# Softmax denominators of four units gathered onto 64 partitions before the logarithm, and spread back by DMA

## The chip, the core and the metric

The kernel runs on one core of a Trainium2 chip. Five engines share the work. TensorE (PE in the profile, with PEld for its weight loads) multiplies matrices into PSUM. ScalarE (ACT) evaluates functions such as the exponential. VectorE (DVE) and GpSimd (POOL) do elementwise work. SyncE (SP) issues the DMAs; its instructions, like those of every engine, start in program order. The metric is the device time of one execution in microseconds (us), the median over several runs; less is better.

## The reference

The function is one transformer block. With x of 2048 tokens and 512 features, c a conditioning vector and LN a layer norm without weights:

```python
mod = silu(c) @ w_mod            # six vectors: sa, ca, ga, sb, cb, gb
h = LN(x) * (1 + ca) + sa
x = x + ga * A(h)                # A: attention, 32 heads of 16, causal, window of 256 tokens
h = LN(x) * (1 + cb) + sb
x = x + gb * B(h)                # B: LN, then an MLP that mixes tokens: 2048 -> 1792 -> 2048
```

In the attention the scores are scaled by 1/4, masked to the 256 keys up to the query, and softmaxed; the result times the values goes through the 512 x 512 matrix wo. What concerns this document is the division of the softmax: each head and query has one sum of exponentials (its denominator), and the head's 16 outputs are divided by it.

## The kernel before

**Tiles and units.** The 2048 tokens are taken as four groups G of 512. A unit is half a group (256 queries, number H = 0 to 7) and a quarter of the features (g8 = 0 to 3, which is 8 heads, 128 partitions): 32 units, named (H, g8) below. The scores of the units are cut into 75 chunks of 4 x 512 columns, numbered 0 to 74. For a chunk `S` multiplies keys with queries into PSUM: three banks (`pss`, one buffer) and a fourth bank (`psb`, two buffers). `EA` and `EB` are the exponentials of the three banks and of the fourth on ScalarE, into an `et` tile of a ring of E_BUFS = 7. `M` multiplies by the mask on VectorE. When the last chunk of a unit is masked, the `AV` operations sum the unit in PSUM: `unit["ps"][:, 0, :]` gets the exponentials times the values, and `unit["ps"][:, 1, :]` gets their plain sums through the matrix of ones `ones_bd`, so that the sum of a head stands on all 16 partitions of that head.

**The division.** `finish` ends a unit. ScalarE takes the logarithm of the 128 x 256 sums out of PSUM (`ln`) and the exponential of its negative (`rz`), and VectorE multiplies (`OT`). Since a head's 16 partitions hold the same sum, each value is worked out 16 times:

```python
ac.activation(out=unit["lz"][:], in_=unit["ps"][:, 1, :], func=ACT.Ln)
ac.activation(out=unit["lz"][:], in_=unit["lz"][:], func=ACT.Exp, scale=-1.0)
ve.tensor_tensor(out=OT..., in0=unit["ps"][:, 0, :], in1=unit["lz"][:], op=ALU.mult)
```

The bank of the unit is one of three (`od0` to `od2`) that all dense products use in turn; it is held until `OT` is done.

**Work beside the attention.** `proj` makes the keys, queries and values of the next group (normalized tiles `xn`, DMA transposes `xt` into `h1T`, products `k`, `q`, `v`, copies `ke`, `qe`, `ve` out of PSUM, `kk`, `vo`, `vp` that place them). `post` takes a finished group through wo (`wo`), the residual (`x2`) and the two norms into `hb`. `partials` starts the first product of the MLP with what is there of hb (`p`, w1 loaded as `w1a` to `w1d`), and `tail` ends it (`u`, Gelu `g`) and runs the second product (`py`). `mod_ops` are the six vectors' use: four of them are broadcast to 128 partitions by products with a replicated silu(c) (`bc`) and copied out of PSUM (`bce`).

**The order.** Every operation is an `Op` with engines it may run on, a planned cost, dependencies and extra landing time. `ORDER` is a list of the operations' numbers, the result of a search; `CHOSEN` gives the engine of those that may run on two. `run_schedule` emits them in that order, so on each engine, and on SP's queue of DMAs, they run in the order of the list. SP waits at a DMA whose data is not ready, and what follows it in the list waits with it.

The names that the change touches: `finish`, `mod_ops`, `E_BUFS`, the tiles `hb`, `nothing`, `kb`, `vb`, `vs`, `sT_rep`, the operation `rel` (which frees the pool with the first weights), `ORDER` and `CHOSEN`. Most instructions are issued through one helper, so that their line is L256 in the profile; they are told apart by the tiles they write and read.

Of the kernel before, what the change touches and what calls it, by code (L numbers as in the profile page):

```python
# [59 lines left out]
E_BUFS = 7  # L60
LOG = None
ORDER = [
# [153 lines left out]
def kernel(  # L216
# [324 lines left out]
    for n, (v, dst) in enumerate(((2, bc_ga), (4, bc_cb1), (3, bc_sb), (5, bc_gb))):  # L541
        def e_bc(n, v=v):
            if n == 0:
                box["bc", v] = bank([P, D], F32, "ps_b")
# [32 lines left out]
    def norm_ops(tag, tiles, deps, poss, key, quiet):  # L577
# [32 lines left out]
        if quiet:  # L610
            return op(f"{tag}ag", "POOL", 3.1, e_ag, deps=st_ops, pos=poss[-1])
# [823 lines left out]
```

## Time and profile before

| | |
|---|---|
| time, three runs | 253.68, 253.95, 254.43 us; median 253.95 |
| span of the profiled execution | 252.3 us, first to last instruction |
| median less that span | 1.65 us |
| busy: PE, DVE, ACT, POOL | 235.3, 205.4, 179.5, 126.3 us |
| DMA | 28.13 MB, 39.4% of 16 engines' span on SP's queue |
| granted TensorE clock | 1.00 |

The profile gives the span of its execution, and no other time for it; the time of a run is the longer of the two, by what lies before the first and after the last instruction. The busy time of an engine says how long it worked, not whether the end waits for it. For that one reads the chain that ended last, the time between two like instructions of an engine, and the busy time by stretches of the span. A duration in the rows is that of one instruction from start to end; the next one of the same engine can start before that end, so the distance of two starts is often shorter.

### The profile page before, as it was taken

To read this page: it belongs to the slowest core of one execution; us is meant where nothing else is said; L and a number is where in the kernel's file an instruction comes from. 1 tells how busy PE (TensorE), PEld (TensorE's weight loads), DVE (VectorE), ACT (ScalarE), POOL (GpSimd) and SP (SyncE) were. 2 spreads that over 40 slices of the span, in tenths; PEclk is the share of its full clock that TensorE was granted. 3 is DMA by queue.
4 is the path that set the end of the run, shared out by engine and by line. 5 is a ranking of instruction groups with operands and counts; after the bars stand their busy time and mean duration, and the time that the engine had idled before them with its cause. 6 is when DMAs were issued, how large, how long until landed. Compare 5 with 4: busy or idle time off the path is not lost.

```text
span 252.3 us, 9189 instructions
## 1 busy us (share of the span) xinstructions
PE 235.3 (93%) x3949; PEld 126.0 (50%) x3949; DVE 205.4 (81%) x408; ACT 179.5 (71%) x254; POOL 126.3 (50%) x228
## 2 busy tenths in 40 slices
PE   7988888899987889999999999999999999999995
PEld 2656644445554544555546454556444444444443
DVE  5499998989989998999897999999978764444443
ACT  4699998999999999999999999997147510000000
POOL 8268968795899989845886348173000000000000
PEclk9999999999999999999999999999999999999999
DMA  6999364356055200003401536314999201111111
GB/s 200 323 351 294 48 47 86 44 70 187 3 74 112 53 23 3 4 3 104 131 3 45 155 82 189 105 44 113 343 388 386 108 22 43 44 52 52 42 44 42
DMA packets 42625, 28.13 MB, mean 111 GB/s; under 512 B 12376, under 2 KB 38488, under 8 KB 42584
## 3 DMA queue, kind: packets, MB, share of 16 engines
q1 hardware_dynamic: 42576, 27.54, 39.4%
q8 instruction: 31, 0.51, 0.9%
q14 instruction: 10, 0.08, 0.1%
q10 hardware_dynamic: 8, 0.00, 0.0%
HBM read 22.03 MB, written 2.10 MB: 96 GB/s over the span
## 4 chain that ended last, share of the span: by engine, by line
PE 52%; ACT 24%; DVE 7%; DMA 5%; issue 5%; POOL 4%; SPq 1%; POOLq 0%; DVEq 0%
ACT et L256 20%; PE py L256 19%; PE pu L256 16%; PE po L256 5%; PE pss L256 5%; ACT lz L256 3%; PE pa L256 3%; DMA x<-in_A_x_dram 2%; DVE et L256 2%; DMA h1T<-xn 2%; DMA wmod<-in_w_mod_dram 1%; POOL h1T L256 1%; PE pq L256 1%; DVE st L256 1%; PE pk L256 1%
## 5 line engine op out<-in xcount | busy, mean ns | idle before, releaser
L256 ACT ACTIVATE et<-pss 128x1536 bf16<-128x1536 f32 x75 | 110.7, 1476 | 2.8 <-PE psb L256 2.3
L256 PE MATMUL py<-guT,w2r 128*128 128x512 bf16 (+2 forms) x238 | 48.7, 366 | 0.0
L256 ACT ACTIVATE et<-psb 128x512 bf16<-128x512 f32 x75 | 46.9, 626 | 0.0
L256 DVE TENSOR_TENSOR et<-et,maskt 128x1024 bf16<-128x1024 bf16 (+2 forms) x79 | 46.4, 603 | 0.1
L256 PE MATMUL pu<-hb,w1s 128*32 128x512 bf16 (+1 forms) x302 | 39.0, 380 | 0.2 <-DVE QT L256 0.2
L256 PEld LDWEIGHTS <-w2r 128*128 128x128 bf16 x238 | 22.8, 98 | 26.1 <-issue 0.3
L256 PE MATMUL pss<-QT,KT 32*128 32x64 bf16 (+3 forms) x720 | 29.9, 230 | 6.2 <-ACT et L256 3.5
L256 PE MATMUL po<-et,VT 128*32 128x64 bf16 (+3 forms) x960 | 32.2, 234 | 1.3 <-DVE kb L256 0.6
L256 PE MATMUL po<-et,ones_bd 128*32 128x256 bf16 (+3 forms) x624 | 31.7, 268 | 0.0
L256 PEld LDWEIGHTS <-KT 32*128 32x128 bf16 x960 | 17.1, 92 | 28.5 <-issue 24.6
L256 DVE TENSOR_TENSOR otile<-py,xr 128x512 bf16<-128x512 f32 (+2 forms) x17 | 11.2, 660 | 24.4 <-PE py L256 24.2
L256 POOL TENSOR_SCALAR KT<-kb,mask_par 128x512 bf16<-128x512 bf16 (+1 forms) x36 | 25.0, 707 | 11.4 <-DVE kb L256 11.1
L256 PE MATMUL psb<-QT,KT 32*128 32x64 bf16 (+3 forms) x240 | 29.3, 231 | 0.0
L256 PEld LDWEIGHTS <-VT 128*32 128x32 bf16 x960 | 20.8, 96 | 13.2 <-issue 4.7
L256 PE MATMUL pk<-h1T,wqkv 128*32 128x512 bf16 (+4 forms) x228 | 21.1, 340 | 2.4 <-DVE OT L256 1.0
L256 DVE BATCH_NORM_STATS2 st<-x 128x6 f32<-128x512 bf16 x32 | 21.5, 680 | 2.1 <-DMA x<-in_A_x_dram 2.1
L256 PEld LDWEIGHTS <-wqkv 128*32 128x32 bf16 (+1 forms) x350 | 15.3, 96 | 12.7 <-issue 4.7
L256 PEld LDWEIGHTS <-w1s 128*32 128x32 bf16 (+1 forms) x302 | 14.1, 97 | 15.0 <-issue 1.5
L256 PE MATMUL pv<-wqkv,h1T 128*32 128x512 bf16 (+2 forms) x202 | 17.1, 348 | 1.3 <-DVE OT L256 0.7
L256 PE MATMUL pu<-hb,w1r 128*128 128x512 bf16 (+1 forms) x96 | 17.9, 380 | 0.0
L256 PE MATMUL pa<-wod,OT 128*32 128x512 bf16 (+1 forms) x136 | 17.2, 381 | 0.0
L256 PEld LDWEIGHTS <-ones_bd 128*32 128x32 bf16 x624 | 15.8, 97 | 0.1
(109 smaller groups left out, 350.1 us busy)
## 6 DMA issues: line engine op xcount, KB each, us to landing
w2r<-in_B_w_dram SPq DMA_DIRECT2D x14, 512.0 KB, 10.2
w1s<-in_B_w_dram SPq DMA_DIRECT2D x19, 256.0 KB, 4.0
w1r<-in_B_w_dram SPq DMA_DIRECT2D x9, 256.0 KB, 4.3
x<-in_A_x_dram SPq DMA_DIRECT2D x16, 128.0 KB, 5.2
wmod<-in_w_mod_dram SPq DMA_DIRECT2D x4, 512.0 KB, 7.8
out_dram<-otile SPq DMA_DIRECT2D x15, 128.0 KB, 1.7
wmod<-in_w_mod_dram SPq DMA_DIRECT2D x4, 256.0 KB, 3.9
wqkv<-in_A_wqkv_dram SPq DMA_DIRECT2D x4, 256.0 KB, 5.7
```

Source lines behind the costliest of these rows:

```text
L256: ins = call(*args, **kwargs)
```

## The change

The division is done for four units at once. `ev` copies a unit's whole PSUM tile (sums and products, 128 x 512 float32) into SBUF, on VectorE or ScalarE. `zg`, a DMA, takes every eighth partition of the sums (16 rows, one KB each) into 16 rows of a tile `zc`. When four units are in (64 rows), one `ln` and one `rz` work on those 64 x 256. `zb`, a DMA a unit, spreads the 16 rows to 128 partitions again, and `OT` multiplies from SBUF, on VectorE or GpSimd. There are seven such batches of four units and one of two; the last two units, (7,2) and (7,3), keep a logarithm and exponential of their own. `zc` has two halves in turn, and the `ev` tiles are a ring of six.

```diff
     def finish(unit, i):
         G, Hh, g8 = unit["G"], unit["H"], unit["g8"]
         av = av_ops[G, g8] = unit["avs"][-1]
-        lz_tag = turn("lz")
-
-        def e_ln(e):
-            unit["lz"] = late.tile([P, HQ], F32, name="lz", tag=lz_tag, bufs=1)
-            ac.activation(out=unit["lz"][:], in_=unit["ps"][:, 1, :], func=ACT.Ln)
-
-        def e_rz(e):
-            ac.activation(out=unit["lz"][:], in_=unit["lz"][:], func=ACT.Exp, scale=-1.0)
+        tag = turn("ev", EV_BUFS)
+        direct = Hh == 2 * NG - 1 and g8 >= 2
+        members = box.setdefault("batch", [])
+
+        def e_new():
+            unit["ev"] = kvpool.tile([P, 2, HQ], F32, name="ev", tag=tag, bufs=1)
 
         def e_o(e):
-            ve.tensor_tensor(
+            ENGINE[e].tensor_tensor(
                 out=OT[G % 2][g8][:, (Hh % 2) * HQ : (Hh % 2 + 1) * HQ],
-                in0=unit["ps"][:, 0, :], in1=unit["lz"][:], op=ALU.mult,
+                in0=(unit["ps"] if direct else unit["ev"])[:, 0, :], in1=unit["ev"][:, 1, :], op=ALU.mult,
             )
 
-        a = op("ln", "ACT", 0.26, e_ln, deps=[av], pos=i + LZ_POS)
-        b = op("rz", "ACT", 0.31, e_rz, deps=[a], pos=i + LZ_POS)
-        d = mult_ops[Hh, g8] = op("OT", "DVE", 0.34, e_o, deps=[b], pos=i + OT_POS)
-        unit["avs"][0].frees = [d]
-        slot(lz_tag, a, d)
+        if direct:
+            def e_ln(e):
+                e_new()
+                ac.activation(out=unit["ev"][:, 1, :], in_=unit["ps"][:, 1, :], func=ACT.Ln)
+
+            def e_rz(e):
+                ac.activation(out=unit["ev"][:, 1, :], in_=unit["ev"][:, 1, :], func=ACT.Exp, scale=-1.0)
+
+            a = op("ln", "ACT", 0.26, e_ln, deps=[av], pos=i + LZ_POS)
+            b = op("rz", "ACT", 0.31, e_rz, deps=[a], pos=i + LZ_POS)
+            d = mult_ops[Hh, g8] = op("OT", "DVE", 0.34, e_o, deps=[b], pos=i + OT_POS)
+            unit["avs"][0].frees = [d]
+            slot(tag, a, d)
+            return
+
+        base = KB * (box.setdefault("batches", 0) % 2)
+        rows = slice(base + DH * len(members), base + DH * len(members) + DH)
+
+        def e_ev(e):
+            e_new()
+            copy(e, unit["ev"][:], unit["ps"][:])
+
+        def e_zg(e):
+            dma.dma_start(out=zc[rows, :], in_=unit["ev"][0 : P : P // DH, 1, :])
+
+        def e_zb(e):
+            dma.dma_start(out=unit["ev"][:, 1, :], in_=zc[rows, :].unsqueeze(1).to_broadcast([DH, P // DH, HQ]))
+
+        a = op("ev", {"DVE": 0.6, "ACT": 0.5}, 0.6, e_ev, deps=[av], pos=i + LZ_POS)
+        unit["avs"][0].frees = [a]
+        g = op("zg", "SP", 0.6, e_zg, deps=[a], pos=i + LZ_POS, extra=0.2)
+        members.append((unit, i, tag, a, g, e_o, e_zb))
+        if len(members) < (2 if Hh == 2 * NG - 1 else 4):
+            return
+        own = slice(base, base + DH * len(members))
+
+        def e_bln(e):
+            ac.activation(out=zc[own, :], in_=zc[own, :], func=ACT.Ln)
+
+        def e_brz(e):
+            ac.activation(out=zc[own, :], in_=zc[own, :], func=ACT.Exp, scale=-1.0)
+
+        n = box["batches"]
+        a = op("ln", "ACT", 0.26, e_bln, deps=[m[4] for m in members], pos=i + LZ_POS)
+        for m in members:
+            m[4].deps.extend(tenants.get(f"zc{n % 2}", []))
+        b = op("rz", "ACT", 0.31, e_brz, deps=[a], pos=i + LZ_POS)
+        spread = []
+        for u, at, tag, first, g, e_mult, e_spread in members:
+            z = op("zb", "SP", 1.0, e_spread, deps=[b], pos=at + LZ_POS, extra=0.9)
+            spread.append(z)
+            d = mult_ops[u["H"], u["g8"]] = op("OT", {"DVE": 0.34, "POOL": 0.66}, 0.34, e_mult, deps=[z], pos=at + OT_POS)
+            slot(tag, first, d)
+        tenants[f"zc{n % 2}"] = spread
+        box["batches"] += 1
+        box["batch"] = []
```

The broadcast of the four modulation vectors changes likewise: the four products run on 32 columns of TensorE each, into one bank, one copy takes them out, and four DMAs (`bb`) spread 32 rows to 128 partitions.

```diff
-    for n, (v, dst) in enumerate(((2, bc_ga), (4, bc_cb1), (3, bc_sb), (5, bc_gb))):
-        def e_bc(n, v=v):
-            if n == 0:
-                box["bc", v] = bank([P, D], F32, "ps_b")
-            for k in (2 * n, 2 * n + 1):
+    vectors = ((2, bc_ga), (4, bc_cb1), (3, bc_sb), (5, bc_gb))
+
+    def e_bc(n):
+        if n == 0:
+            box["bc"] = bank([P, D], F32, "ps_b")
+        for k in (2 * n, 2 * n + 1):
+            for i, (v, _) in enumerate(vectors):
                 te.matmul(
-                    box["bc", v][:], lhsT=sT_rep[:, k, :], rhs=wmod[:, k, v * D : (v + 1) * D],
-                    start=(k == 0), stop=(k == ND - 1),
+                    box["bc"][32 * i : 32 * i + 32, :], lhsT=sT_rep[:, k, :], rhs=wmod[:, k, v * D : (v + 1) * D],
+                    start=(k == 0), stop=(k == ND - 1), tile_position=(0, 32 * i), skip_group_check=True,
                 )
 
-        def e_bce(e, v=v, dst=dst):
-            if v == 2:
-                ve.tensor_scalar(
-                    out=dst[:], in0=box["bc", v][:], scalar1=ZSCALE, scalar2=0.0, op0=ALU.mult, op1=ALU.add,
-                )
-            elif v == 4:
-                ve.tensor_scalar_add(out=dst[:], in0=box["bc", v][:], scalar1=1.0)
-            else:
-                ve.tensor_copy(out=dst[:], in_=box["bc", v][:])
-
-        a, z = dense(f"bc{v}", [0.435] * 2, e_bc, [o_rep], 9.0 + n, cls="D", alloc="od", ready=22.0)
-        b = op(f"bce{v}", "DVE", 0.6, e_bce, deps=[z], pos=9.0 + n)
-        a.frees = [b]
-        mod_ops.append(b)
+    def e_bce(e):
+        ve.tensor_scalar(
+            out=bcs[:], in0=box["bc"][:], scalar1=bc_fix[:, 0:1], scalar2=bc_fix[:, 1:2], op0=ALU.mult, op1=ALU.add,
+        )
+
+    bc_first, bc_last = dense("bc", [0.435] * 2, e_bc, [o_rep], 9.0, alloc="od", ready=22.0)
+    bce = op("bce", "DVE", 0.6, e_bce, deps=[bc_last], pos=9.0)
+    bc_first.frees = [bce]
+    for n, (v, dst) in enumerate(vectors):
+        def e_bb(e, n=n, dst=dst):
+            dma.dma_start(out=dst[:], in_=bcs[32 * n : 32 * n + 32, :].unsqueeze(1).to_broadcast([32, ND, D]))
+
+        mod_ops.append(op("bb", "SP", 0.5, e_bb, deps=[bce], pos=9.0 + n, extra=1.0))
```

Room for the new tiles is found by smaller or shared ones, and the order is another:

```diff
-E_BUFS = 7
+E_BUFS = 6
+EV_BUFS = 6
...
 ORDER = [
...
 CHOSEN = {
...
-    hb = [xpool.tile([P, D], BF, name=f"hb{t}") for t in range(NT)]
+    hb = [xpool.tile([P, D], BF, name=f"hb{t}") for t in range(NT - ND)]
...
-    work = att.enter_context(tc.tile_pool(name="work", bufs=2))
...
+            hb.extend(box["B"].tile([P, D], BF, name=f"hb{t}") for t in range(NT - ND, NT))
...
-        released = op("rel", "SP", 0.0, e_rel, deps=[proj_last[NG - 1]], pos=start_of(NG) - 12.0, extra=-2.0)
+        released = op("rel", "SP", 0.0, e_rel, deps=[proj_last[NG - 1], *placed], pos=start_of(NG) - 12.0, extra=-2.0)
+        for o in hb_ops[NG - 1].values():
+            o.deps.append(released)
```

The tiles `kb`, `vb` and `vs` move into the pool `wpool`, and `nothing` (zeros for the warm-up and for clearing VT) into `modw`; both pools are freed during the kernel, so `rel` now also waits for the last placing operations, and `w1open` for the clearing DMAs. Some planned costs are altered: `l1ag` to `l3ag` 3.1 to 3.3, `m2` 0.74 to 0.80 on VectorE and 2.5 to 2.1 on GpSimd, `n2` and `hb` 0.77 to 0.74 on GpSimd.

Counted from the two lists, by operations:

| operation | before | after |
|---|---|---|
| `ln` and `rz`, ACT | 32 and 32 | 10 and 10 |
| `ev`, DVE / ACT | none | 26 / 4 |
| `OT`, DVE / POOL | 32 / 0 | 7 / 25 |
| `zg` and `zb`, SP | none | 30 and 30 |
| `bce`, DVE; `bb`, SP | 4; none | 1; 4 |
| `xn`, DVE / POOL | 7 / 9 | 4 / 12 |
| `ve`, DVE / ACT | 16 / 0 | 14 / 2 |
| first `pe` of the MLP's parts, DVE / ACT | 13 / 1 | 10 / 4 |

Ahead of chunk 40 (the 41st) in the lists there are 16 `ln` and 16 `rz` before, 4 and 3 after; `OT` on DVE 16 before, 2 after; `OT` on POOL none and 9; `ev` on DVE none and 16. Behind the scores of chunk 40 TensorE's list holds 99 dense products of two matmuls each (`k`, `q`, `v`, `wo`, and `p`, `u` of the MLP) before and 102 after, and 48 `AV` operations before and 47 after.

More of the change, by code (lines that the diff above doesn't have):

```diff
@@ L335 @@
     modw = tc.alloc_tile_pool(name="modw", bufs=1, side="right")
-    warm = nothing
+    warm = nothing = modw.tile([P, D], BF, name="nothing")
+    nc.vector.memset(nothing[:], 0.0)
     wmod = modw.tile([P, ND, 6 * D], BF, name="wmod")
@@ L473 @@
     sT = modw.tile([P, ND], BF, name="sT")
-    sT_rep = modw.tile([P, ND, P], BF, name="sT_rep")
+    sT_rep = modw.tile([P, ND, 32], BF, name="sT_rep")
+    bcs = modw.tile([P, D], BF, name="bcs")
+    bc_fix = modw.tile([P, 2], F32, name="bc_fix")
+    nc.gpsimd.memset(bc_fix[:, 0:1], 1.0)
+    nc.gpsimd.memset(bc_fix[0:32, 0:1], ZSCALE)
+    nc.gpsimd.memset(bc_fix[:, 1:2], 0.0)
+    nc.gpsimd.memset(bc_fix[32:64, 1:2], 1.0)
     box = {}
@@ L504 @@
     o5.frees = [o6]
-    o_rep = op("sTrep", "DVE", 0.35, lambda e: ve.tensor_copy(
-        out=sT_rep[:], in_=sT[:].unsqueeze(2).to_broadcast([P, ND, P])), deps=[o6], pos=-6, ready=15.0)
+    o_rep = op("sTrep", "DVE", 0.15, lambda e: ve.tensor_copy(
+        out=sT_rep[:], in_=sT[:].unsqueeze(2).to_broadcast([P, ND, 32])), deps=[o6], pos=-6, ready=15.0)
     def e_fm(k):
@@ L652 @@
     transposed = {}
+    placed = []
     def proj0():
@@ L1045, in post @@
             a.frees = [x_ops[tl]]
-        engine, shifted = ({"POOL": 0.77, "DVE": 0.35}, True) if G < POOL_POST else ({"DVE": 0.34}, False)
+        engine, shifted = ({"POOL": 0.74, "DVE": 0.33}, True) if G < POOL_POST else ({"DVE": 0.34}, False)
         st = norm_ops("l2", lambda i: xres[4 * G + own[i]], [[x_ops[tl]] for tl in own],
```

23 lines of the change are left out of this document (12 added, 11 removed), and 129 rows, old and new, of tables (CHOSEN, ORDER).

## The prediction

> **What bounds the kernel now.** I read the page first (who is busy, and when), then the busy time by stretches, then the chain that ended last, then ScalarE's instructions one after the other.
>
> ```profile
> span 252.3 us, 9189 instructions
> ...
> PE   7988888899987889999999999999999999999995
> ...
> ACT  4699998999999999999999999997147510000000
> ```
>
> ScalarE is at 8 or 9 tenths from the 3rd slice to the 27th, TensorE at 9 from the 16th (95 us) to the 39th. So there are two stages: one in which the exponentials set the pace, and one, from about 95 to 120 us on, in which TensorE has more than it can do. By stretches (columns: length, then busy us and count of PE, PEld, DVE, ACT, POOL, then clock, DMA share, GB/s), cut at the first exponential (11.22), at that of chunk 40 (98.43), and at the end of the attention:
>
> ```profile
> 11.22:98.43 87.21, 76.76 (x1793) 45.36 (x1793) 82.08 (x167) 85.31 (x116) 71.88 (x122) 1.00 0.48 106
> 98.43:119.17 20.74, 19.63 (x468) 10.98 (x468) 19.85 (x38) 20.72 (x28) 14.11 (x22) 1.00 0.11 31
> 119.17:161.90 42.73, 42.27 (x913) 22.62 (x911) 38.77 (x70) 42.27 (x58) 26.42 (x47) 1.00 0.39 107
> 161.90:178.50 16.60, 16.60 (x357) 9.51 (x354) 16.38 (x37) 13.49 (x24) 6.86 (x11) 1.00 0.32 87
> 178.50:252.30 73.80, 70.98 (x342) 32.75 (x340) 42.94 (x81) 12.23 (x20) 0.00 (x0) 1.00 0.35 128
> ```
>
> Stage 1 (87.21 us): ScalarE 97.8% busy, VectorE 94.1%, TensorE 88.0%, GpSimd 82.4%. Stage 2, the 153.87 us behind it: TensorE is idle 1.11, 0.46 and 0 us up to 178.50. Its end is therefore the start of chunk 40 plus TensorE's work left then.
>
> Busy is not yet the price of an instruction on ScalarE. The chain shows what a chunk waits for:
>
> ```profile
> 97.99 0.29 PE pss L256 x3
> ...
> 98.44 1.45 ACT et L256
> ...
> 99.93 0.26 PE pss L256 x3
> ```
>
> There is one buffer of three banks, so a chunk's scores start when the exponential before has left it, and the next exponential starts when they are in: 1.45 us and some 0.5 us of TensorE in a ring. ScalarE's fourth-bank exponential fits into that 0.5 us:
>
> ```profile
> 16.53 1.45 ACT L256 ACTIVATE et<-pss 128x1536 bf16<-128x1536 f32 x1
> 17.87 0.59 ACT L256 ACTIVATE et<-psb 128x512 bf16<-128x512 f32 x1
> 18.47 1.45 ACT L256 ACTIVATE et<-pss 128x1536 bf16<-128x1536 f32 x1
> ...
> 48.76 1.50 ACT L256 ACTIVATE et<-pss 128x1536 bf16<-128x1536 f32 x1
> 50.09 0.66 ACT L256 ACTIVATE et<-psb 128x512 bf16<-128x512 f32 x1
> 50.56 0.46 ACT L256 ACTIVATE lz<-po 128x256 f32<-128x256 f32 x1
> 50.83 1.53 ACT L256 ACTIVATE et<-pss 128x1536 bf16<-128x1536 f32 x1
> 52.16 0.51 ACT L256 ACTIVATE lz<-lz 128x256 f32<-128x256 f32 x1
> 52.47 0.69 ACT L256 ACTIVATE et<-psb 128x512 bf16<-128x512 f32 x1
> 52.94 1.55 ACT L256 ACTIVATE et<-pss 128x1536 bf16<-128x1536 f32 x1
> ```
>
> From exponential to exponential: 1.94 us with nothing beside them, 2.07 with a logarithm, 2.11 with its exponential. A unit's pair costs 0.13 + 0.17 = 0.30 us of pace, not the sum of its durations, since part of it lies in the gap that the scores need anyway.
>
> **The change part by part.** The rows that price it (group: count, busy us, mean ns, idle before):
>
> ```profile
> L256 ACT ACTIVATE lz<-lz 128x256 f32<-128x256 f32 x32 | 14.1, 450 | 0.1
> L256 ACT ACTIVATE lz<-po 128x256 f32<-128x256 f32 x32 | 13.0, 405 | 0.7 <-PE po L256 0.5 <-DVE OT L256 0.2
> L256 DVE TENSOR_TENSOR OT<-po,lz 128x256 bf16<-128x256 f32 x32 | 13.2, 415 | 2.4 <-ACT lz L256 1.9
> L256 DVE COPY part<-pu 128x512 f32<-128x512 f32 x13 | 8.8, 678 | 0.3 <-PE pu L256 0.2
> L256 ACT ACTIVATE part<-pu 128x512 f32<-128x512 f32 x1 | 0.6, 600 | 0.0
> L256 DVE TENSOR_SCALAR bc_cb<-ps_b 128x512 bf16<-128x512 f32 x1 | 0.7, 673 | 0.0
> L256 PE MATMUL ps_b<-wmod,sT_rep 128*128 128x512 bf16 x16 | 4.1, 380 | 0.0
> L256 POOL TENSOR_TENSOR h<-h,bc_cb 128x512 bf16<-128x512 bf16 x4 | 5.3, 1328 | 4.1 <-DVE h L256 4.0
> L256 DVE TENSOR_TENSOR et<-et,maskt 128x1024 bf16<-128x1024 bf16 x43 | 31.8, 742 | 0.1
> ```
>
> *ScalarE.* By busy time 22 pairs go, 22 x 0.855 = 18.8 us. By pace, stage 1 loses 12 of 16 pairs: 12 x 0.30 = -3.6 us. Two value copies come onto ScalarE there, as large as the 0.60 us copy; each lengthens a chunk by between 0.13 (what the shorter logarithm costs) and 0.60, I take 0.37, the middle: +0.7. Together -2.9: the ring alone would allow 84.3 us.
>
> *VectorE.* Sixteen units' copies come, each as the 128 x 512 float32 copy: 16 x 0.678 = +10.8. Fourteen multiplications leave: 14 x 0.415 = -5.8. Three of four broadcast copies leave: 3 x 0.673 = -2.0. The other pieces that change engine (three `xn`, two `x2`, two `ve` fewer, two `h1T` and one `kk` more, and smaller ones) come to between -4 and 0; each is 0.4 to 0.7 us, like the rows above, and I take -2.8. Sum +0.2: 82.3 us, 97.6% of the 84.3. VectorE did 95.7% in the stretch after 98.43 and 98.7% in the last 16.6 us of the attention, but nothing near that over 80 us. At 95.7% stage 1 takes 86.0. I take 85.0 (96.8%), between that and the ring: **-2.2 us**, bounds -2.9 and +0.3 (VectorE at the 94.1% of today).
>
> *GpSimd.* Nine multiplications of stage 1 at half of the 1.33 us of its 512-wide product: 9 x 0.66 = 5.9 (up to 12 if float32 costs it double); with three more `xn` and other pieces some +7.4: 79.3 of 85.0 us, 93%. It is not the bound, but the 18% of air that it had is 7%; nothing is charged, and what is late then are keys and values of the next group.
>
> The Trainium skill ("SBUF — State Buffer", Who interferes with whom) says that a VectorE operation with two SBUF inputs and a GpSimd operation that reads SBUF exclude each other: whichever comes second waits out the whole instruction. It speaks against moving 25 multiplications to GpSimd; by it each could hold a mask product for its full length, which is the second rival below. The trace agrees in kind, with a small sum: the 43 wide masks average 742 ns, and this one alone is
>
> ```profile
> 58.36 0.68 DVE L256 TENSOR_TENSOR et<-et,maskt 128x1024 bf16<-128x1024 bf16 x1
> ```
>
> so 43 x 0.06 = 2.7 us were lost beside the 119 us that GpSimd is busy in the stretches above; 5.9 us more of it add 0.1.
>
> *TensorE.* The broadcast products run four abreast: 4.1 us become about 1.0, in stage 1, where TensorE is not the bound: 0. Behind chunk 40's scores the new list leaves three dense products more and one `AV` less. From the chain, four matmuls of a dense product, and the 52 that sum a unit in three `AV`:
>
> ```profile
> 128.29 0.86 PE pk L256 x4
> ...
> 132.63 1.10 PE po L256 x52
> ```
>
> 3 x 0.43 less 1.10 / 3 is **+0.9 us** of work in stage 2, bounds 0 and +1.3 (the `AV` not counted). TensorE's idle 1.6 us there could shrink: the bank of a unit is let go after one copy and no longer held through logarithm, exponential and multiplication. I take none of it (bounds 0 and -1.6).
>
> *DMAs.* They are on SP:
>
> ```profile
> w1s<-in_B_w_dram SPq DMA_DIRECT2D x19, 256.0 KB, 4.0
> ...
> out_dram<-otile SPq DMA_DIRECT2D x15, 128.0 KB, 1.7
> ...
> vs<-vb SPq DMA_DIRECT2D x24, 32.0 KB, 1.9
> ...
> 44.89 1.14 SPq L256 DMA_DIRECT2D vs<-vb  x2
> ```
>
> Between issue and landing 1.7 to 1.9 us; 64 issues at 0.57 are 36 us of a queue that now issues one thing every few us. A gather stands ahead of `ln` on ScalarE, and behind that `ln` are the next exponentials: if the sums are late, the pace stops. In the new list most `ln` stand a chunk or more (1.94 us) behind the last gather, which is just its landing. I charge **+0.3** for eight batches, bounds 0 and 8 x 2.1 (a gather behind a w1 load, 4.0 instead of 1.9). Spreading hides behind the four or more chunks before `wo`; if GpSimd's multiplication waits for it, `kk`, `vo` and `xn` wait behind. The `bb` DMAs land 20 us before their first reader: 0. Six `et` buffers for seven: no row shows an exponential waiting for sums; 0, up to one chunk's 1.94. `rel` later: the w1 loads behind it are covered by products whose weights are in; without that cover one landing, 4.0.
>
> **Sum.** 252.3 - 2.2 + 0.9 + 0.3 = 251.3 us of span. The median of the runs is 253.95, 1.65 more than the span: **252.9 us** (251.3 + 1.65), 0.4% less than before. (About 0.3%, 0.76 us, is what can be told from no change.)
>
> **The rivals.**
> *VectorE keeps its 94.1%.* The pace is then not ScalarE's at all: 82.3 / 0.941 = 87.5, +0.3, and the +0.9 of TensorE and +0.3 stay: 253.8, time 255.4. For it: its many small waits are for others' results, and copies add more of them. Against it: 98.7% in the last stretch.
> *GpSimd's multiplications hold the masks.* Place: VectorE in stage 1. If each of the nine holds one for 0.66, VectorE has 88.2 us, at the 96.8% of the forecast 91.1: +3.9 + 0.9 + 0.3, 257.4, time 259.1. It decides where stage 1 passes 86.0 us (87.2 less the 1.2 that stage 2 and the landings add), from 83.2 us of VectorE work: 0.9 us held, 0.1 a multiplication. Against it: the 0.06 a mask above.
> *Sums land late.* From chunk 33 the new list has w1 loads between the gathers. If four batches wait the 2.1 us and TensorE's stored products cover half, +4.2: 255.5, time 257.2. For it: the load's 4.0. Against: the distance in the list.
> *Nothing comes of it:* gains and losses cancel within 0.3%, 253.2 to 254.7.
>
> **How the numbers follow.** Forecast (249.5 to 253.2; the lower end is 252.3 - 2.9 + 0 - 1.6 + 0 + 1.65 from the bounds, the upper is 0.3% below the median) 0.42; cancelled 0.15; VectorE as today 0.16; sums late 0.15; masks held 0.12. So faster 0.42, same 0.15, slower 0.43. The range 249.5 to 257.5 leaves out the masks held at their full price and the sums late by more than half. The forecast's own range is 249.5 to 253.2.
>
> **What would show it.** Ten `ln` of which eight read `zc`, most chunk distances at 1.94 to 1.96; chunk 40's exponential at 95 to 97 instead of 98.43; VectorE above 95% up to there; GpSimd about 93%; TensorE still without idle from 120 us, and its stage behind chunk 40 about 154.8 us. I am wrong if `ln` shows idle time ended by a DMA, if masks grow well above 742 ns, if GpSimd's late keys or values end TensorE's waits, or if the new multiplications cost GpSimd much more than 0.66.

## The result, and the profile after

| | before | after |
|---|---|---|
| median of the runs | 253.81 us (253.51 to 254.43) | 267.97 us (267.39 to 268.51) |
| ratio to before | 1 | 1.055, 95% interval 1.0517 to 1.0584 |
| span of the profiled execution | 252.3 us | 266.1 us |
| busy PE, DVE, ACT, POOL | 235.3, 205.4, 179.5, 126.3 us | 236.2, 217.4, 175.5, 153.7 us |

The change made the kernel 5.5% slower; the forecast was 252.9 us, the range 249.5 to 257.5. ScalarE lost 4 us of work, VectorE got 12 and GpSimd 27. Two executions of g2 and one of g4 below were over 1.5% longer than the fastest of the same kernel; they are left out, and g4, whose profile fell in such an execution, has no line in the table of stretches. From the page of the changed kernel (span, 40 equal slices, then the chain that ended last):

```profile
span 266.1 us, 9254 instructions
...
ACT  4399999959954799999997999997416640000000
...
PEclk9799999999997799999999999999999999999999
...
PE 34%; DVE 25%; POOL 18%; issue 5%; ACT 4%; DMA 3%; SPq 1%; DVEq 0%; POOLq 0%; ACTq 0%
```

Before, ScalarE's slices were 8 or 9 from the 3rd to the 27th; now there are holes in the 9th and from the 12th to the 14th, and in the 13th and 14th TensorE's clock is down to 0.7. The chain ran 52% on TensorE and 24% on ScalarE before; it now runs 25% on VectorE and 18% on GpSimd, and 4% on ScalarE.

The stretches by busy time (columns as in the prediction), cut at the first exponential, at that of chunk 40, and 1.45 us behind the start of the last wide exponential; first the kernel before, for the two last cuts, which the prediction cut elsewhere:

```profile
98.43:171.76 73.33, 71.75 (x1602) 39.06 (x1605) 68.41 (x126) 72.72 (x97) 46.41 (x80) 1.00 0.27 75
171.76:252.30 80.54, 77.72 (x478) 36.80 (x470) 49.52 (x98) 16.00 (x32) 0.97 (x1) 1.00 0.38 131
```

The changed kernel:

```profile
12.98:106.00 93.02, 74.50 (x1754) 44.77 (x1756) 83.87 (x156) 81.08 (x93) 78.94 (x127) 0.96 0.48 109
106.00:182.87 76.87, 70.85 (x1554) 38.77 (x1553) 74.71 (x123) 72.86 (x84) 60.70 (x95) 1.00 0.46 102
182.87:266.10 83.23, 80.11 (x519) 38.15 (x508) 52.05 (x100) 16.66 (x31) 6.80 (x9) 1.00 0.41 139
```

So stage 1 grew by 5.8 us (87.21 to 93.02), the rest of the attention by 3.5 and the end by 2.7; 1.8 us lie ahead of the first exponential. That start differs from one profiled execution to another: the first exponential came at 11.0 to 13.4 us in the kernel before and six made from it, and at 11.5 to 13.0 in the changed kernel and four made from it. So the runs are compared by the stretches behind it as well as by time. Three runs below (e3, e4, g3) do extra work at the start, where their first exponential comes at 14.3 to 15.3 us.

Most of stage 1's loss is one place. The changed kernel's ScalarE and then SP, around chunk 30:

```profile
75.12 1.45 ACT L260 ACTIVATE et<-pss 128x1536 bf16<-128x1536 f32 x1
76.47 0.59 ACT L260 ACTIVATE et<-psb 128x512 bf16<-128x512 f32 x1
83.53 0.42 ACT L260 ACTIVATE zc<-zc 64x256 f32<-64x256 f32 x1 [6.47 <-DMA zc<-ev]
83.85 1.43 ACT L260 ACTIVATE et<-pss 128x1536 bf16<-128x1536 f32 x1
```

```profile
64.69 2.28 SPq L260 DMA_DIRECT2D vs<-vb  x2
72.17 1.22 SPq L260 DMA_TRANSPOSE h1T<-xn  x1
73.50 0.56 SPq L260 DMA_DIRECT2D zc<-ev  x1
74.11 2.10 SPq L260 DMA_TRANSPOSE h1T<-xn  x1
76.26 1.22 SPq L260 DMA_DIRECT2D vs<-vb  x2
77.52 0.59 SPq L260 DMA_DIRECT2D zc<-ev  x1
78.16 2.67 SPq L260 DMA_TRANSPOSE h1T<-xn  x2
80.93 1.16 SPq L260 DMA_DIRECT2D zc<-ev  x2
```

The logarithm of the third batch waits 6.47 us for gathers, and the exponentials of chunks 30 and 31 stand behind it on ScalarE. The gathers left SP at 73.50, 77.52 and 80.93 though VectorE's last copies for them ended at 72.6: SP was held by a transpose whose `xn` GpSimd had ready only at 72.15, and by three more. That is not the list's order. The list has: gather of (3,0), transpose `xt3.3`, spill `vx2_0`, gathers of (2,0), (2,1), (3,1), then the operation `w1` (number 996, which frees a pool), then spill `vx2_1` and transposes `xt3.2`, `xt3.1`, `xt3.0`. In the compiled program DMAs that were emitted behind the release of a pool stand, at four places, ahead of DMAs emitted before it: here `vx2_1` and `xt3.2` at the head and `xt3.1`, `xt3.0` ahead of two gathers; later a w1 load ahead of a gather, and the first w2 load ahead of w1 loads. The other engines keep the list's order, and in the kernel before SP did too. That the release of the pool is the reason is read from these places; no run shows it.

Two groups of VectorE in the kernel before, then the moved work and the same two in the changed kernel (groups; then a DMA issue: count, KB each, median us to landing):

```profile
L256 DVE TENSOR_TENSOR h<-h,bc_sb 128x512 bf16<-128x512 bf16 x12 | 6.0, 500 | 0.4
...
L256 DVE TENSOR_TENSOR h<-h,bc_cb 128x512 bf16<-128x512 bf16 x12 | 5.4, 448 | 0.9 <-POOL h L256 0.8
```

```profile
L260 POOL TENSOR_TENSOR OT<-ev 128x256 bf16<-128x256 f32 x25 | 21.5, 876 | 2.1 <-DMA ev<-zc 1.8
L260 DVE COPY ev<-po 128x512 f32<-128x512 f32 x26 | 17.5, 680 | 2.3 <-PE po L260 1.0
L260 DVE TENSOR_TENSOR h<-h,bc_sb 128x512 bf16<-128x512 bf16 x11 | 8.1, 732 | 0.4
L260 DVE TENSOR_TENSOR h<-h,bc_cb 128x512 bf16<-128x512 bf16 x11 | 7.0, 639 | 0.0
...
zc<-ev SPq DMA_DIRECT2D x30, 16.0 KB, 1.8
```

### The profile page after: what moved, and what is told of

Same layout as the page of the kernel before. It is cut to its first block, busy times and chain, and to the rows that moved or that the text cites. A ratio compares the mean times of both kernels' runs of the same rounds, so it can differ in the third digit from the quotient of the medians.

```text
span 266.1 us, 9254 instructions
## 1 busy us (share of the span) xinstructions
PE 236.2 (89%) x3901; PEld 127.5 (48%) x3901; DVE 217.4 (82%) x399; ACT 175.5 (66%) x217; POOL 153.7 (58%) x261
## 4 chain that ended last, share of the span: by engine, by line
PE 34%; DVE 25%; POOL 18%; issue 5%; ACT 4%; DMA 3%; SPq 1%; DVEq 0%; POOLq 0%; ACTq 0%
PE py L260 18%; PE pu L260 10%; DVE et L260 6%; DVE st L260 4%; DVE h L260 4%; ACT et L260 4%; POOL KT L260 3%; POOL h L260 3%; DVE part L260 3%; POOL VT L260 3%; POOL xn L260 2%; DVE ev L260 2%; PE pa L260 2%; POOL OT L260 2%; PE pss L260 2%
## 5 line engine op out<-in xcount | busy, mean ns | idle before, releaser
L260 ACT ACTIVATE et<-pss 128x1536 bf16<-128x1536 f32 x75 | 108.8, 1451 | 6.1 <-PE psb L260 3.0
L260 DVE TENSOR_TENSOR et<-et,maskt 128x1024 bf16<-128x1024 bf16 (+2 forms) x79 | 47.8, 628 | 5.2 <-ACT et L260 5.1
L260 ACT ACTIVATE et<-psb 128x512 bf16<-128x512 f32 x75 | 44.5, 595 | 0.1
L260 PEld LDWEIGHTS <-KT 32*128 32x128 bf16 x960 | 18.3, 93 | 39.1 <-issue 35.6
L260 POOL TENSOR_SCALAR KT<-kb,mask_par 128x512 bf16<-128x512 bf16 (+1 forms) x34 | 23.4, 702 | 10.8 <-ACT kb L260 6.5
L260 PEld LDWEIGHTS <-VT 128*32 128x32 bf16 x960 | 21.5, 98 | 15.7 <-issue 7.1
L260 POOL TENSOR_TENSOR OT<-ev 128x256 bf16<-128x256 f32 x25 | 21.5, 876 | 2.1 <-DMA ev<-zc 1.8
L260 PE MATMUL pv<-wqkv,h1T 128*32 128x512 bf16 (+2 forms) x184 | 17.8, 355 | 2.4 <-DVE ev L260 2.4
L260 DVE COPY ev<-po 128x512 f32<-128x512 f32 x26 | 17.5, 680 | 2.3 <-PE po L260 1.0
```

Of the source, the lines that this page charges most:

```text
L260: ins = call(*args, **kwargs)
```

## The experiments

Four theories came up, in this order. A: gathers held on SP stop ScalarE. B: GpSimd and VectorE have too much to do. C: VectorE is the bound behind chunk 40. H (D for stage 2): the places in the list keep engines waiting, whatever the load. Other letters belong to one or two runs alone. The table gives the profiled executions by stretches, so that the start drops out: stage 1, rest of the attention, end, and their sum. Times and ratios are in the text.

| kernel | stage 1 | rest | end | sum |
|---|---|---|---|---|
| before | 87.21 | 73.33 | 80.54 | 241.1 |
| after | 93.02 | 76.87 | 83.23 | 253.1 |
| e1 SP as listed | 86.14 | 77.68 | 82.81 | 246.6 |
| e2 sums aside | 88.95 | 79.55 | 82.85 | 251.4 |
| e3 narrow multiplications | 90.05 | 75.63 | 81.62 | 247.3 |
| e4 = e1 + e3 | 85.75 | 75.79 | 81.58 | 243.1 |
| f1 = e1 + half masks | 87.84 | 77.87 | 81.68 | 247.4 |
| f2 before + half masks | 87.32 | 73.34 | 80.45 | 241.1 |
| f3 before + VectorE copies | 86.74 | 78.72 | 80.40 | 245.9 |
| f4 = e1 + work moved | 87.35 | 84.81 | 82.84 | 255.0 |
| g1 before + GpSimd products | 88.85 | 79.05 | 81.57 | 249.5 |
| g2 before + 60 DMAs | 90.88 | 73.33 | 80.35 | 244.6 |
| g3 = e4 + half masks + sums aside | 86.58 | 75.18 | 81.31 | 243.1 |
| h1 before + broadcast part | 86.84 | 73.34 | 80.28 | 240.5 |
| h2 before, 9 of 32 pairs | 86.14 | 72.85 | 80.19 | 239.2 |

### SP in the order of the list

```diff
                 if pinned[0]:
                     tc.keep_in_program_order(ins)
+                    if self.engine is nc.sync:      # and behind the DMA emitted last
+                        if last[0] and last[0] != ins.ins.name:
+                            tc.add_manual_dep(ins.ins, last[0], <order only, no wait>)
+                        last[0] = ins.ins.name
```

> The changed kernel with one thing different: SP issues its DMAs in the order of the written list. (In the changed kernel as compiled, four DMAs that the list has later stand ahead of gathers and of w1 and w2 loads: among them the value spill and the transpose of which the second waits for GpSimd's xn until 72.17 us, so that the gathers of the third batch leave SP at 77.52 and 80.93 although their copies were done at 72.5.) Theory A (gathers held on SP): the logarithm of that batch, 83.53 us now, starts at 76.5 to 78, TensorE's clock stays at 1.00 there, chunk 30 starts 5 to 7 us earlier and chunk 40 at 98 to 100; the time is 259 to 262.5. Rival B (GpSimd and VectorE have too much to do; SP only shows it): the logarithm's wait is followed by a wait for keys, values or norms of about the same length; the time stays within 2 us of 268.

Measured: 262.67 us, 1.036 of before (1.032 to 1.0405), 5.3 below the changed kernel. SP and ScalarE of this run:

```profile
68.66 1.22 SPq L261 DMA_TRANSPOSE h1T<-xn  x1
...
72.21 1.87 SPq L261 DMA_DIRECT2D zc<-ev  x3
74.12 1.63 SPq L261 DMA_DIRECT2D vs<-vb  x2
75.86 3.84 SPq L261 DMA_TRANSPOSE h1T<-xn  x3
```

```profile
77.01 0.42 ACT L261 ACTIVATE zc<-zc 64x256 f32<-64x256 f32 x1
77.33 1.43 ACT L261 ACTIVATE et<-pss 128x1536 bf16<-128x1536 f32 x1
```

The gathers leave right behind the copies, the logarithm runs at 77.01 without a wait, chunk 30 starts 6.5 us earlier (77.33) and chunk 40 at 99.11, with the clock at 1.00. A is shown for this place, and worth 5.3 us of the 14 (6.5 between the two profiled executions, by the stretches); the time lies 0.2 us above what A expected, the marks in the trace lie where it expected them. What is left is elsewhere:

```profile
12.97:99.11 86.14, 71.83 (x1746) 44.10 (x1756) 83.06 (x156) 81.03 (x94) 78.17 (x125) 1.00 0.53 119
99.11:176.79 77.68, 70.57 (x1558) 38.85 (x1563) 75.76 (x123) 72.85 (x84) 61.54 (x99) 1.00 0.45 101
```

With SP as listed stage 1 is 1.07 us shorter than before, VectorE at 96.4% of it. Behind chunk 40 VectorE has 75.76 us of work in place of 68.41, the stretch is 4.35 longer, and TensorE, 97.8% busy there before, is at 90.8%.

### No logarithm waits for a gather

```diff
-            dma.dma_start(out=zc[rows, :], in_=unit["ev"][0 : P : P // DH, 1, :])
+            dma.dma_start(out=aside[4 * Hh + g8], in_=unit["ev"][0 : P : P // DH, 1, :])   # in device memory
```

> The changed kernel (its compiled SP order too), but the gathers write to a buffer that nobody reads, and the logarithm runs on rows set to one; so all DMAs and all ScalarE work stay, and no logarithm waits for a landing. (The division is by other numbers.) Theory A (late sums stop ScalarE): the waits of 6.5 and 2.6 us and the half clock behind the first are gone, and the smaller ones at chunks 39 to 41; time 256 to 260. Rival B (GpSimd and VectorE overloaded): the exponentials run on and then wait for masks, sums, keys or norms instead; 264 to 268.

Measured: 264.59 us (ratio 1.039 to 1.047). B's figure, not A's. The waits of 6.5 and 2.6 us are gone, and TensorE waits for VectorE's copies instead: from 56 to 104 us

```profile
PE po L260 <- DVE kb L260: 3.2, 1, 3.2
PE po L260 <- DVE vb L260: 1.3, 1, 1.3
```

SP's order was still the compiled one, so value spills and transposes stood where they did. So the held logarithm is not the whole price of the compiled order.

### The multiplications on 16 columns

```diff
+            n = HQ if direct else DH
             ENGINE[e].tensor_tensor(
-                out=OT...[:, (Hh % 2) * HQ : (Hh % 2 + 1) * HQ], in0=(...)[:, 0, :], in1=unit["ev"][:, 1, :], op=ALU.mult,
+                out=OT...[:, (Hh % 2) * HQ : (Hh % 2) * HQ + n], in0=(...)[:, 0, :n], in1=unit["ev"][:, 1, :n], op=ALU.mult,
             )
```

(The `OT` tiles are set to one at the start, by VectorE. In e4 this is

```profile
1.00 4.27 DVE L327 MEMSET OT<- 128x512 bf16 x8
```

and the first exponential starts at 14.28 us, in e1 at 12.97.)

> The changed kernel (its compiled SP order too), but the multiplications of the batched units work on 16 columns in place of 256 (the rest of their output is left at one), so that GpSimd is relieved of about 25 x 0.7 = 17 us and VectorE of 5 x 0.3 us, with every wait kept. Theory A: only the one or two multiplications ahead of the xn that the transposes wait for matter (1.8 us at 69.61); the logarithm still waits 3 to 5 us; time 263 to 267. Rival B: GpSimd is the chain from 38 to 97 us, and a sixth of its work is gone: 254 to 261.

> Both of the runs before at once: SP as listed and the multiplications on 16 columns. Theory A: what the listed SP order leaves of the loss (5 to 8 us over the kernel before) is in landings, in VectorE's copies and in the end of the attention, not in GpSimd's multiplications: within 2 us of the run with the SP order alone. Rival B: 5 us or more below the run with the SP order alone, 253 to 257.

Measured: 263.79 us (1.037 to 1.049), and with SP as listed 260.51 (1.0233 to 1.031). By time the first is in A's range, not in B's, and the second lies 2.2 us under e1, just outside A's 2 and far from B's 5. But both pay for setting the tiles. Behind the first exponential e4 is 3.5 us shorter than e1: 0.4 in stage 1, 1.9 in the rest and 1.2 in the end.

```profile
100.03:175.82 75.79, 71.25 (x1575) 39.41 (x1580) 73.21 (x126) 72.85 (x84) 53.51 (x98) 1.00 0.47 104
```

There the change costs 12.0 us (253.1 to 241.1). SP's order takes 6.5 of them away, the multiplications 3.5 more, and 2.0 are left. So the multiplications, 25 on GpSimd and five on VectorE, are the larger part of what SP's order leaves there, which is nearer to B than the time alone shows.

### Is VectorE the bound behind chunk 40?

```diff
             def e_mask(e, i=i, masks=masks):
+                js = 2 if i >= 40 else 4          # of the four banks, those that are masked
```

> The kernel with SP as listed (262.7 us), and from chunk 40 on the masks are multiplied onto two of the four score banks only (the other two stay unmasked), which takes some 8 to 10 us off VectorE and leaves everything else. With SP as listed, stage 1 (first exponential to chunk 40) took 86.1 us, the rest of the attention 77.7 (73.3 in the kernel before) with VectorE 97.5% busy and TensorE 90.8%. Theory C (VectorE's added work in stage 2 is the bound there): the stretch from chunk 40 to the last exponential falls to 72 to 74.5 us, time 257 to 260. Rival D (late landings and the list's order hold stage 2, VectorE is only full because it can be): 76 us or more, time 261 to 263.

> The control: the kernel before with the same halved masks from chunk 40 on (two of the four banks stay unmasked). Theory C: there TensorE is the bound of stage 2 (97.8% busy), so the relief of VectorE brings under 1 us: 252.7 to 253.8. Rival D: VectorE's relief is worth about the same in both kernels, 2 us or more: 250 to 252.

And the opposite, work added to the kernel before:

```diff
             ve.tensor_tensor(out=OT..., in0=unit["ps"][:, 0, :], in1=unit["lz"][:], op=ALU.mult)
+            if Hh in (4, 5, 6):
+                for _ in range(2):
+                    ve.tensor_copy(out=unit["lz"][:], in_=unit["lz"][:])
```

> The other way round: the kernel before, with two extra VectorE copies of 128 x 256 float32 in place behind the multiplication of each of the twelve units of heads 4 to 6 (stage 2), some 8 to 10 us of VectorE work that nobody waits for but the next operation on VectorE. Theory C: VectorE goes from 68.4 to about 77.5 us in a stretch of 73.3, so the stretch must grow to 78 or more and the time by 4 to 6 us: 258 to 260. Rival D: VectorE has 4.9 us of air there, most of the copies fall into it: under 2 us, 254 to 255.5.

Measured: f1 260.31 us (1.0213 to 1.0294), f2 253.80 (0.9978 to 1.0045), f3 259.05 (1.0175 to 1.0263). f3 is C's: VectorE goes from 68.41 to 75.33 us, and the stretch from 73.33 to 78.72:

```profile
98.48:177.20 78.72, 72.06 (x1592) 39.31 (x1605) 75.33 (x151) 73.84 (x97) 45.79 (x80) 1.00 0.25 70
```

So 6.9 us more on VectorE cost 5.4 on the list of the kernel before; the 7.35 that the change added there could by that account for its 4.35. By the groups of that stretch in e1 the 7.35 are ten copies `ev` (6.8 us, less 3.0 for multiplications that left and 2.0 for three `part` copies), operations that were there before and got longer: the 21 wide masks by 1.85 us, four pairs of scale and shift products, which take 2.7 us more than five did, and about 1.0 us of smaller pieces. f2 is C's too: relief is worth nothing in the kernel before. But f1 is not:

```profile
99.35:177.22 77.87, 72.70 (x1574) 39.89 (x1582) 71.31 (x126) 73.04 (x84) 56.54 (x100) 0.98 0.46 101
```

The masks gave VectorE back 4.5 us (75.76 to 71.31, not the 8 to 10 that I had expected), and the stretch did not get shorter (77.68 to 77.87; C had 72 to 74.5, D 76 or more). Some 1.2 us of that are a slow clock (below). So f3 shows that such work on VectorE can cost this much on the old list; that it is what holds the changed kernel is not shown, and f1 speaks against it. By time f1 lies between C's 257 to 260 and D's 261 to 263, 2.4 us under e1, which its profiled execution does not show; that stays open.

### Work moved off VectorE

Five copies `ev` of stage 2 go to ScalarE, two multiplications to GpSimd, by `CHOSEN` alone.

> SP as listed, and in stage 2 five sum copies (of units (5,0), (5,1), (4,3), (6,1), (7,0)) go from VectorE to ScalarE and two multiplications ((4,0), (5,0)) from VectorE to GpSimd, at their places in the list. VectorE loses 5 x 0.68 + 2 x 0.8 = 5.0 us there, ScalarE gains 3.0 and some of its pace. Theory C: stage 2 falls from 77.7 to 75 to 76 (VectorE at 97%: 73; ScalarE's pace takes part of it back), time 260 to 261.5. Rival D: 262 to 264, since copies on ScalarE make the exponentials later and nothing else changes.

Measured: 268.58 us (1.0555 to 1.0649). Neither theory. ScalarE's waits in this run:

```profile
ACT ev L242 <- POOL OT L242: 4.5, 1, 4.5
```

A copy needs a free `ev` slot, of which there are six; the multiplication that frees it was now behind keys on GpSimd, and on ScalarE the exponentials stood behind the copy. This is the gather's stall with another cause: what can be late stood ahead of the exponentials.

### The parts alone, on the kernel before

```diff
+            po.tensor_tensor(out=idle[:, 0, :], in0=idle[:, 0, :], in1=idle[:, 1, :], op=ALU.mult)   # at 25 units: g1
+            dma.dma_start(out=aside[4 * Hh + g8], in_=idle[0 : P : P // DH, :])                      # at 30 units: g2
+            dma.dma_start(out=apart[4 * Hh + g8], in_=idle[0:DH, :].unsqueeze(1).to_broadcast([DH, P // DH, HQ]))
```

> One part alone: the kernel before, with one extra GpSimd product of two 128 x 256 float32 tiles (nobody reads it, and it waits for nothing but GpSimd) at the place of each of the 25 multiplications that the change moves to GpSimd; VectorE keeps its own. Theory E (GpSimd's added work costs by holding VectorE and by making keys and norms late): 25 x 0.73 to 0.88 = 18 to 22 us more on GpSimd, VectorE's products and h1T lengthen as in the changed kernel, time 256 to 259. Rival F (GpSimd has the air, as the prediction had it): within 1 us of the kernel before.

> One part alone: the kernel before, with 30 transfers of 16 rows and 30 broadcasts of 128 KB issued by SP at the places of the multiplications, from a constant tile to memory that nobody reads, so that they wait for no engine and nobody for them. Theory E: the queue and the transfers as such cost little, within 1 us of the kernel before; what costs is what waits for a landing. Rival G (SP's queue and the DMA engines are the price): value spills, transposes and weight loads land later, 256 us or more.

Measured: g1 264.22 us (1.0338 to 1.0438), above even what E expected. 25 products that nobody waits for cost 9.8 us over the kernel before in the same session (254.41), 8.4 of them behind the first exponential. From the groups and stretches of g1:

```profile
L256 POOL TENSOR_TENSOR idle<-idle 128x256 f32<-128x256 f32 x25 | 20.4, 817 | 0.7
...
L256 DVE TENSOR_TENSOR h<-h,bc_cb 128x512 bf16<-128x512 bf16 x12 | 7.6, 631 | 1.5 <-POOL h L256 1.5
L256 DVE TENSOR_TENSOR h<-h,bc_sb 128x512 bf16<-128x512 bf16 x12 | 7.3, 610 | 0.4
```

```profile
13.43:102.28 88.85, 77.20 (x1792) 45.54 (x1792) 83.46 (x165) 85.52 (x116) 79.11 (x131) 1.00 0.44 97
102.28:181.33 79.05, 72.62 (x1602) 39.19 (x1605) 72.32 (x128) 73.31 (x96) 58.22 (x94) 1.00 0.25 69
```

VectorE's own work is the same list as before, 408 instructions, and it became 7.3 us longer (205.4 to 212.7 us over the span): the scale and shift products take 631 and 610 ns in place of 448 and 500. Behind chunk 40 it is 3.9 us (68.41 to 72.32), 1.4 of them two copies that now fall behind the cut. GpSimd makes others late as well: the chain of g1 runs 30% on it, where it was 4%. g2: 257.49 and 259.07 us (before 254.41), rival G by time. Its profiled execution, the faster of the two, lost 3.5 us behind the first exponential, all in stage 1 (3.7, less 0.2 in the end) and most of it at one place:

```profile
PE pk L256 <- POOL h1T L256: 2.6, 2, 2.3
```

The transposes of group 1 stood behind the added DMAs on SP, so `h1T` and the keys came late, 2.87 us at chunk 13. Why the other run took 1.6 us more was not seen.

### All reliefs at once, and three places of the list

> All reliefs at once: SP as listed, multiplications of the batched units on 16 columns, masks on two of four banks from chunk 40 on, gathers to a buffer that nobody reads (the division is by other numbers). If the causes named so far (SP's order, GpSimd's multiplications, VectorE's load in stage 2, landings) are all there are, what is left over the kernel before is TensorE's +0.9 to +1.6 and the set-up of the output tiles at the start (1.3): 254 to 256.5. Rival H (the list itself keeps engines waiting, with any load): 258 or more.

```diff
 # in ORDER, of e1
-  225 (ln of the second batch), 757, 334, 372 (S21), 373 (EA21), 226 (rz)
+  757, 334, 372, 373, 225, 226
-  591 (M37), 601, 770, 260 (l3st0.0), 574 (ke2_3)
+  591 (M37), 574, 601, 770, 260
-  500 (m2_1.2), 695 (ev(4,3)), ... 708 (ev(5,3)), ... 820 (qe3_3)
+  695, ... 708, ... 820, 500
```

> SP as listed, and three places of the list changed with no work changed: the logarithm of the second batch goes behind the exponential of chunk 21 in place of ahead of it; the key copy ke2_3 ahead of the statistics l3st0.0 (chunk 39); on VectorE the scale and shift m2_1.2 behind the copies ev(4,3), ev(5,3) and the query copy (chunk 57). Rival H (places in the list): 1.9, 0.6 and 1.9 us of the waits at chunks 21, 39 to 41 and 57 to 59 go, time 258 to 260. Theory C (VectorE full, a place freed is a place lost): the waits come back within a few chunks, time within 1.5 us of 262.7.

Measured: g3 259.67 us (1.0144 to 1.0261): by time H, 258 or more. But its first exponential starts at 15.33 us, 4.1 later than in the kernel before; only 2.0 us are lost behind it, as in e4 (243.1 both), and the expectation had 0.9 to 1.6 there from TensorE's work alone. So by the stretches the causes named account for 10 of the 12 us, and H for little. The rest of its attention:

```profile
101.91:177.09 75.18, 72.24 (x1583) 39.36 (x1581) 67.55 (x126) 72.94 (x84) 49.10 (x99) 1.00 0.47 105
```

VectorE has less to do there than before the change (67.55 to 68.41 us), and the stretch is 1.85 us longer; 0.5 of that is TensorE's added work (72.24 to 71.75). What remains may belong to the new list; no run separates it. g4: 261.65 us (260.34 to 263.68; 1.0214 to 1.0379). C's figure, within 1.5 us of e1; the interval is too wide to tell it from a gain of 2 us. Three places mended brought nothing that can be told.

### What there was to gain

```diff
+        own = g8 == 3 or Hh == 2 * NG - 1 and g8 == 2     # h2: these keep their pair, the others multiply by ones
```

> The most that the change could gain: the kernel before with 9 of its 32 pairs of logarithm and exponential (units of the fourth group of each head, and (7,2)); the other units are multiplied by ones (so they are not divided), with no copy, DMA or GpSimd work added. Theory P (the prediction's ring: 12 pairs fewer in stage 1 at 0.30 us each, and none of it in stage 2 where TensorE is the bound): stage 1 falls from 87.2 to 83.6 to 84.3, time 250 to 251. Rival S (VectorE, at 94.1% of stage 1, and the keys and values set the pace there, not ScalarE): stage 1 86 or more, time 252.5 to 254.

> One part alone: the kernel before with the new way to lay out the four modulation vectors (products four abreast into one bank, one copy, four broadcast DMAs), at the places in the list where the four old copies stand. TensorE loses about 3 us of work there and VectorE 3 x 0.67 = 2.0 us. Theory P (as predicted: neither is the bound where it happens): within 0.8 us of the kernel before. Rival Q (VectorE's 2 us come through, since it is 94% busy in stage 1): 251.5 to 253. Rival R (the four transfers on SP hold a transpose, as 60 transfers did): 255 or more.

Measured: h2 252.33 us (0.9922 to 0.999), h1 255.01 (1.0015 to 1.0067). h2 is S's: with 23 of 32 pairs gone and nothing added, stage 1 is 86.14 us, not 83.6 to 84.3:

```profile
11.32:97.46 86.14, 76.69 (x1793) 44.82 (x1793) 81.66 (x167) 80.34 (x92) 71.78 (x122) 1.00 0.49 107
```

ScalarE is then 93.3% busy, VectorE 94.8%. Most chunks do not come at 1.94 us when the pairs are gone: ahead of the next scores TensorE has other products, and some of these wait for VectorE (the key products at 73.90 for 1.21 us, for a bank that `OT` frees). 13 of the 39 distances of stage 1 are under 1.97 us, 7 before the change, and 17 in e1. So the most that the pairs could bring, on this list, is 1.1 us by the ratio (0.44% of 253.8; 0.3 to 2.0 by its interval, 1.9 by the stretches). h1 misses P's 0.8 us and just reaches R's 255, but not by R's mechanism: its stretches are no longer than before, and what it lost lies ahead of the first exponential (12.54 us), where executions differ by as much.

Nothing here points to a kernel that beats the one before.

## Why the prediction was wrong, step by step

Two steps of the prediction failed above all: that the gathers land in time (+0.3), and that GpSimd has room for the multiplications (nothing charged). Of the 14 us, 12.0 lie behind the first exponential. Taking the causes away one after the other in the changed kernel gives 6.5 for SP's order (e1; 5.3 by the medians), 3.5 for the multiplications (e4, the 25 on GpSimd and five on VectorE together), and 2.0 that stay, and that lighter masks and no wait for sums do not lower (g3). Each figure is from one profiled execution; executions of one kernel differ by up to 2 us (e1: 261.73 to 263.85). In g3 TensorE has 1.3 us more to do behind chunk 40 than before the change, near the +0.9 that was forecast. The other 2 us of the 14 lie ahead of the first exponential and outside the span. The parts alone on the kernel before have the sizes 8.4 (GpSimd's products), 4.8 (VectorE, in f3's form), 3.5 (DMAs) and -1.9 (pairs); they are measured on a list that was not searched for them, so they give sizes and no account.

- **"I charge +0.3 for eight batches" (failed).** The landing itself was as taken, 1.8 us. The distance in the list was no guide, because SP did not issue in the order of the list: one `ln` waited 6.47 us. The bound, 8 x 2.1, was for a gather behind a load; what it stood behind was a transpose behind GpSimd. The document's own sentence, that SP's queue runs in the order of the list, was true of the kernel before and was not looked at for the other. With the order restored (e1) the time falls by 5.3 us, and one batch still waits, 2.5 us at chunk 21. With the compiled order but no wait of a logarithm (e2) it falls by 3.4, so the term's own share is smaller than that of the order.
- **"Stage 1 -2.2" (half of it, with SP as listed).** e1 has -1.07, inside the bounds -2.9 and +0.3. VectorE: forecast 82.3 us at 96.8%, measured 83.06 at 96.4%.
- **"The ring alone would allow 84.3" (not borne out).** 0.30 us a pair was read from chunks where a pair stood beside the ring. h2 took 23 pairs away, 12 of them in stage 1, and gained 1.07 us there, not 2.9 to 3.6: 0.09 us a pair. A difference of two distances is the price of a pair only if nothing else ends the wait the moment the pair is gone.
- **"VectorE" (incomplete: stage 2 was left out).** The sum counted the copies of stage 1. Behind chunk 40 ten more stand on VectorE, and its work there grew by 7.35 us in a stretch where it had 4.9 us of air; TensorE, which I took for the only bound there, then waits for copies. The term was 0 in the sum. Its size in the changed kernel is not shown: f3 gives 5.4 us on the old list, but in e4 all ten copies are still there and the stretch is 2.5 us over the kernel before, 1.85 in g3.
- **"Nothing is charged" for GpSimd, and 0.1 for holding VectorE (failed).** 0.66 us a multiplication measured 0.876 in the mean, 0.72 to 0.73 where nothing held it (g1). I priced contention by the wide masks and by what they lost before. They grew from 742 to 757 ns (822 in e1), and VectorE's scale and shift products went from 448 and 500 ns to 639 and 732. g1 prices this part alone at 9.8 us on the old list; in the changed kernel it is 3.5 behind the first exponential, with VectorE's five (e4 under e1). Rival two had the mechanism, though not in the masks of stage 1 first of all, and its 259.1 is less than this part alone in g1.
- **"TensorE +0.9" (nearly right).** Its work behind chunk 40 is 70.85 + 80.11 = 150.96 us, before 71.75 + 77.72 = 149.47: +1.5, a little over the bound of 1.3; +1.3 in g3. That it would be the only bound there is what failed.
- **"The `bb` DMAs: 0" (open).** h1 is 0.15 to 0.67% slower, and its trace does not say where beyond the start. Six `et` buffers alone were not tried.
- **Rival three, "sums land late" (right in kind).** It gave 257.2 with a w1 load as the cause. One late batch waited three times the assumed time (6.47 to 2.1 us), TensorE stood still for 5.1 us beside and behind it, and its clock was at half for 6.8 us.

## What to carry to other kernels

Before you price a wait from a list, read in what order the queue really issues: here spills and transposes stood ahead of gathers that the list had first. Take the relieved work away alone first: it showed a ceiling of 1 to 2 us for a change that puts 12 and 27 us on two engines which were 94% and 82% busy. Price added work in every stage of the kernel, and on the engine beside it too. When a run that takes a cause away adds work of its own, compare it behind that work: by time alone e4 and g3 read the other way.

## What the runs showed of the hardware

**VectorE beside GpSimd.** In e1, VectorE's row and then GpSimd's at the same time:

```profile
132.38 1.38 DVE L261 TENSOR_TENSOR h<-h,bc_cb 128x512 bf16<-128x512 bf16 x1
133.79 1.26 DVE L261 TENSOR_TENSOR h<-h,bc_sb 128x512 bf16<-128x512 bf16 x1
```

```profile
132.27 1.20 POOL L261 TENSOR_TENSOR h<-h,bc_cb 128x512 bf16<-128x512 bf16 x1
133.55 1.22 POOL L261 TENSOR_TENSOR h<-h,bc_sb 128x512 bf16<-128x512 bf16 x1
```

The product that takes VectorE 0.42 us at its shortest (417 ns in the mean of five in the kernel before, behind chunk 40) takes 1.26 to 1.38 beside two GpSimd products: each starts 0.1 to 0.2 us after GpSimd's and ends 0.3 us after it. The Trainium skill ("SBUF — State Buffer", Who interferes with whom) says that the second to come waits out the other's whole instruction; these rows agree, and the price is what was left of GpSimd's instruction (1.1 and 1.0 us), not a share of it. The prediction averaged it over the masks and got 0.06.

**The clock after a short idle time.** In the changed kernel TensorE stood still for 5.1 us up to 85.3, and its clock fell:

```profile
80.00:82.00 2.00, 0.21 (x8) 0.09 (x1) 1.78 (x3) 0.00 (x0) 1.86 (x4) 1.00 0.37 76
82.00:84.00 2.00, 0.00 (x0) 0.00 (x0) 0.00 (x0) 0.47 (x2) 1.59 (x7) 0.77 0.06 16
84.00:86.00 2.00, 0.67 (x20) 0.47 (x23) 0.00 (x0) 2.00 (x4) 1.81 (x4) 0.50 0.00 0
```

The Trainium skill ("TensorE: Matmul & The Clock Gate", Part 1) names an idle window of some 3.4 us for this. The whole idle time here is longer than that, but the clock fell at 83.1, 2.9 us behind the last product. And in f1 the clock was at 0.50 from 99.2 to 102.6 after an idle time of 2.52 us, shorter than that; e1 had 2.53 us at the same place and kept 1.00. So an idle time of 2.5 us cost 1.2 us more in one execution (from chunk 40 to 43 it took 7.45 us in f1, 6.28 in e1) and nothing in the other. The start differs in the same way: in the changed kernel and in e1 the clock was at 0.50 for 3.4 us from about 8 us on, in f1 it was not, and its first exponential came 1.5 us earlier.
